# Gate sums by 128-column products, a bf16 zero state, and filler products moved to the head of the kernel

## The chip, the cores and the metric

The kernel runs on one core of one Trainium2 chip. The metric is the device time of one execution in microseconds (us); the time before is the median of three runs.

## What is computed

Two layers follow each other. The first is a gated recurrent attention (mLSTM) over 4 batches, 8 heads, 768 steps and head size 40; the second is a feed-forward layer over 3072 tokens, 320 to 2048 to 320, with a hard-swish.

```
m_new = maximum(f_gate + m, i_gate)
f_stab = exp(f_gate + m - m_new);  i_stab = exp(i_gate - m_new)
C = f_stab * C + i_stab * v k^T;   n = f_stab * n + i_stab * k
y = sigmoid(o_gate) * (C q) / max(|n q|, 1)
...
h = x @ w_in;  g = h * clip(h + 3, 0, 6) / 6;  out = g @ w_out
```

## The kernel before

**The attention** works in chunks of 128 steps, each cut in two halves of 64 (Q). In place of the step-by-step recurrence, running sums of the gates are made once per chunk range (`gates`), and a tile of decay factors of 128 x 256 per pair of heads (`gate`), exponentiated on ACT (L688). A `group` on PE makes the scores (part S, L720), the new state contributions (part K, L727) and the outputs (part B: the products with the carried state at L736, and with the weighted scores at L741). VectorE (DVE) and ScalarE (ACT) then finish: `front` (L755) multiplies scores and decay, `state` (L772 to L783) updates the state, `back` (L803, L805) sums the output, `fin` normalizes it, `turn` transposes it for the second layer. Work is cut in tasks: a task is a set of three (chunk, batch) pairs and half the heads. Tasks 0 and 1 have three groups each of kind S+K and of kind B, which use separate PSUM banks (xy, exy).

**The gate tiles of tasks 0 and 1** are not read back from memory as those of later tasks, but summed on PE (L662 to L667): an identity times a causal mask in bf16, and a selector matrix `sel` times the running sums in fp32. The two halves of the partitions are made by separate products, 64 columns each (`rows`), so that a half uses a quarter or less of the array. An fp32 product appears in the trace as two instructions.

**A state that doesn't exist yet** (first chunk of a batch) is read from a tile of fp32 zeros (`zero`, L730), with the same products as a real one. Eight B groups do that.

**The second layer** starts when the early pools are released (`open_moe`, event "mo"): `mm1` (L952) and `mm2` (L996 to L1000), with three fp32r products in place of one fp32. Its weights come packed and are decoded first on ACT and DVE (`weight_slice`, L866 to L911).

**The order of work** is fixed at build time: `Plan.run` steps through all jobs with costs of its own and due times, and each job writes its instructions as its step is reached. Each engine then runs its list in order, also SyncE (SP), which issues all DMAs. The plan's clock is not that of the chip. `T_WARM` (6.9) and `TF` (18.5) are times of the plan.

**Fillers.** The job `warm` has the last rank on PE: where the plan finds PE idle, from 18.5 on its clock until "mo", it writes one bf16 product of 128 x 512 zeros from the tile `ones` into a bank that nothing reads (L460). `ones` is cleared by GpSimd (POOL) as its first job (L455). POOL then makes `sel`, the mask and the identity with memsets and affine selects (L482 to L492), before its first step of the gates (L498).

Of the kernel before, what the change touches and what calls it, by code (L numbers as in the profile page):

```python
# [7 lines left out]
F32 = mybir.dt.float32  # L8
F32R = mybir.dt.float32r
BF16 = mybir.dt.bfloat16  # L10
# [4 lines left out]
ALU = mybir.AluOpType  # L15
# [4 lines left out]
L = 128  # L20
# [5 lines left out]
BH = B * H  # L26
BR = 2 * BH
E2 = D + 2
Q = 64
# [53 lines left out]
WN = 512  # L83
# [4 lines left out]
BL = 2.781  # L88
T_WARM = 6.9
TF = 18.5121  # L90
ENGINES = 'yddzwagdyxdadgddaapddddgyagadx'
BG = -2.7305
BA = -12.8028
# [78 lines left out]
class Plan:  # L172
# [4 lines left out]
    def __init__(self, slots):  # L177
        self.free = {e: 0.5 for e in "padgq"}
        self.free["a"] = 2.5
        self.dma = 0.5  # L180
        self.slots = {k: [(0.0, i) for i in range(n)] for k, n in slots.items()}
        self.done = {}
        self.jobs = []
        self.behind = {}
        self.held = {}
        self.opened = []
        self.nw = 0
        self.work = {}
        self.port = 0.0
        self.small = False  # L190
        self.shared = {}
        self.n = 0

    def add(self, due, gen, after=(), att=1, slack=None):
        self.n += 1
# [101 lines left out]
    def run(self):  # L297
        self.settle()
        while self.jobs:
            best = {}  # L300
            for j in self.jobs:
                e = j["req"][0]
                cost = j["req"][1]
                if e == "*":
                    fin = {o: self.ready(j, o, c) + c + {"a": BA, "d": BD, "g": BG}[o] for o, c in j["req"][1].items()}
                    e = min(fin, key=fin.get)
                    cost = j["req"][1][e]
                if e not in self.free:
                    continue
                start = self.ready(j, e, cost)  # L310
                if e == "p":
                    start = max(start, j["t"] + HOPP * (j["eng"] != e and j["att"]))
                if e == "q" and not j["first"]:
                    start = max(start, self.dma - BL)
                late = start > max(self.free[e], self.port if (e == "g" or isinstance(cost, Lock)) else 0.0) + j["slack"]
                k = (late, start if late else 0.0, j["due"] + (j["req"][2] if len(j["req"]) > 2 and e != "q" else 0.0), j["n"])
                if e not in best or k < best[e][0]:
                    best[e] = (k, start, j, e, cost)
            assert best, [(j["n"], j["due"], j["req"]) for j in self.jobs]
            _, start, j, e, cost = min(best.values(), key=lambda b: b[1])  # L320
            if e == "q":
                self.free[e] = start + (j["req"][2] if len(j["req"]) > 2 else 0.475)
                self.dma = max(self.dma, self.free[e] + DMA0) + cost
                j["t"] = self.dma + DMA
            else:
                end = start + cost
                if e == "p":
                    big = j["gen"].__name__ in ("mm1", "mm2")
                    if big and self.small:
                        cost = cost + 0.08  # L330
                    self.small = not big
                    end = self.stream(start, cost)
                elif e == "g" or isinstance(cost, Lock):
                    self.port = end
                self.free[e] = j["t"] = end
            j["eng"] = e
            self.resume(j, e)
            self.settle()
        assert not self.nw, list(self.behind)

# [36 lines left out]
def mlstm_moe_kernel(ctx: ExitStack, tc: tile.TileContext, ig, fg, qkd, natd, ond, w_in, w_out, ident_d, out):  # L377
    nc = tc.nc
# [16 lines left out]
    ones = cst.tile([128, max(WN, 128)], BF16, name="ones")  # L395
    half = cst.tile([128, 1], F32, name="half")
    mask = cst.tile([128, Q], F32, name="mask")
    zero = cst.tile([128, 2, E2], F32, name="zero")
# [5 lines left out]
    f_s = cst.tile([BR, GN * L], F32, name="f_s")  # L404
# [13 lines left out]
    plan = Plan(dict(wm=1, ez=0, xy=1, exy=1, z=1, es=1, eo=1, st=2, nat=2, gw=NGW, ht=2, on=1, x=2,  # L418
                     y=NY, raw=NRAW, lw=2, mm=2, acc0=1, acc1=1, acc2=1, g=2, gs=GS, ob=3, rd=3))
    put, event = plan.put, plan.event  # L420
    early, early_ctx = {}, {}
# [29 lines left out]
    def warm():  # L451
        got = yield "get", "wm"
        pw = early["ps"].tile([128, 512], F32, tag="wm", name="pw")
        yield "g", 0.1
        nc.gpsimd.memset(ones, 0.0)  # L455
        while "mo" not in plan.done:
            plan.now["t"] = max(plan.now["t"], TF)
            yield "p", mat(1, WN, four=False), 1.0e6
            if "mo" not in plan.done:
                nc.tensor.matmul(pw[:, :WN], ones[:, :128], ones[:, :WN], start=True, stop=True)  # L460

    sel = early["ea"].tile([BR, 12, Q], F32, name="sel")
    maskb = early["ea"].tile([128, Q], BF16, name="maskb")
    identb = early["ea"].tile([128, Q], BF16, name="identb")

    def load_ident():
        yield "q", kb(64, 300)
# [3 lines left out]
    def gates(c0, n):  # L471
# [5 lines left out]
        nc.sync.dma_start(f_s[:, :w], fg[:, cols])  # L477
        nc.sync.dma_start(i_s[:, :w], ig[:, cols])
        if c0 == 0:
            nc.vector.memset(one, 1.0)  # L480
            nc.vector.memset(one.rearrange("p (c t) -> p c t", t=Q)[:, :, 0:1], 0.0)
            nc.gpsimd.memset(sel, 1.0)  # L482
            for h in range(2):
                rs = slice(h * BH, h * BH + BH)
                nc.gpsimd.affine_select(sel[rs], sel[rs], pattern=[[-16, 2], [-1, 6], [0, Q]], compare_op=ALU.is_equal, fill=0.0, base=-8 * h, channel_multiplier=1)
            nc.gpsimd.memset(mask, 0.0)
            nc.gpsimd.memset(identb, 1.0)
            for h in range(2):
                rs = slice(h * Q, h * Q + Q)
                nc.gpsimd.affine_select(mask[rs], mask[rs], pattern=[[1, Q]], compare_op=ALU.is_ge, fill=NEG, base=0, channel_multiplier=-1)  # L490
                nc.gpsimd.affine_select(identb[rs], identb[rs], pattern=[[1, Q]], compare_op=ALU.is_equal, fill=0.0, base=0, channel_multiplier=-1)
            nc.gpsimd.tensor_copy(maskb, mask)  # L492
        f, i, m = f_s[:, :w], i_s[:, :w], m_s[:, 1 : w + 1]
        yield "d", ld(w)
# [1 line left out]
        b, t = (0 if c0 else 1), plan.now["t"]  # L496
        e = yield psub(26, w)
# [12 lines left out]
        t = plan.now["t"]  # L510
# [24 lines left out]
        e = yield pick(22, a=ca(32 * n), d=cd(32 * n))  # L535
        cast(e, gTs[:, :n], pc[:, 0])
        t = plan.now["t"]
# [33 lines left out]
    Cs = {}  # L571
# [73 lines left out]
    def gate(task, cp):  # L645
# [10 lines left out]
        if task < GBT:  # L656
            yield "wait", f"g_s{c}"
            gb = yield "get", "z", "eo", "ez"
            pb = bank(gb, [128, 2, 2, Q], f"gb{nm}")
            plan.now["t"] = max(plan.now["t"], T_WARM)  # L660
            yield "p", busy(1.0)
            rows = [(slice(h * Q, h * Q + Q), slice(h * BH, h * BH + BH)) for h in range(2)]  # L662
            for ho, _ in rows:
                nc.tensor.matmul(pb[ho], identb[ho], maskb[ho, None, None, :].broadcast_to([Q, 2, 2, Q]), start=True, stop=False)
            for j in range(2):
                for ho, hr in rows:
                    nc.tensor.matmul(pb[ho, j], sel[hr, 6 * quad + 2 * b + j], f_s[hr, c * L : c * L + L], start=False, stop=j == 1)  # L667
            src, slot = pb, gb
        else:
            if cp == 0:  # L670
                yield "wait", f"gsc{pair(u, U - 1)[0]}"
                t0 = plan.now["t"]
                for h in range(2):
                    plan.now["t"] = t0
                    yield "q", kb(197, 230), 0.6
                    nc.sync.dma_start(gt[h * Q : h * Q + Q].rearrange("p u j c t -> p (u j c t)"), gsc[quad, h, U * u : U * u + U].rearrange("n j t -> (n j t)")[None, :].partition_broadcast(Q))
                event(f"gl{nm}")
            else:
                yield "wait", f"gl{task}_0"
            e = yield pick(27, g=0.72, d=ld(256))  # L680
            E(e).tensor_tensor(gw, gw, mask[:, None, None, :].broadcast_to([128, 2, 2, Q]), ALU.add)
            src, slot = gw, None
# [16 lines left out]
    def group(g, parts):  # L699
# [9 lines left out]
        for kind, n in parts:  # L709
# [17 lines left out]
                            nc.tensor.matmul(xy[h * Q : h * Q + KM, c, 296 + j * E2 : 296 + j * E2 + E2], T["kn"][rs, o : o + KM], T["vn"][rs, cp, 2 * h + j], start=True, stop=True)  # L727
            else:
                st, gt, vh = T["st"][0], T["gw"][0], T["vh"]
                C0 = Cs.get((b, quad, ch - 1, 1), zero)  # L730
                C1 = Cs[(b, quad, ch, 0)]
                for j in range(2):
                    for h in range(2):
                        rs = slice(h * Q, h * Q + D)
                        for c in range(2):
                            nc.tensor.matmul(xy[c * Q : c * Q + Q, h, 212 + j * E2 : 212 + j * E2 + E2], st[rs, cp, j, 2 if c == h else 4], (C1 if c else C0)[rs, j], start=True, stop=True)  # L736
                for j in range(2):
                    for h in range(2):
# [429 lines left out]
```

## Time and profile before

| | us |
|---|---|
| median of three runs | 467.95 |
| the three runs | 467.95, 466.8, 472.23 |
| profiled execution, device time | 471.43 |
| its span (first to last instruction) | 469.7 |
| PE busy in the span | 456.3 (97%) |
| DVE, ACT, POOL busy | 304.9, 173.3, 179.2 |

The profiled execution took 1.7 us around its span. All times of the trace count from the span's start. PE's busy time is from modelled ends of pipelined products, so that a busy PE isn't one at its peak: the distance from one start to the next says more.

### The profile page before, as it was taken

The numbers are of one execution on the slowest core, as the hardware profiler recorded it, in microseconds if no ns is written. First come the engines' busy times: TensorE is split into PE (matmuls) and PEld (weight loads), VectorE is DVE, ScalarE is ACT, GpSimd is POOL, SyncE is SP. The second block draws the span as 40 slices with busy tenths as digits, with TensorE's granted clock in tenths as the row PEclk, the third lists the DMA queues.
The fourth block names the chain that finished last, engine by engine and source line by source line (L and its number), as shares of the span: only waits on it lengthen the run. The fifth ranks groups of instructions, "written<-read, shape, count | busy, mean of one in ns | idle before, by whom it ended". The sixth has DMA issues, their size and how long they took to land.

```text
span 469.7 us, 12926 instructions
## 1 busy us (share of the span) xinstructions
PE 456.3 (97%) x5407; PEld 419.7 (89%) x5407; DVE 304.9 (65%) x824; ACT 173.3 (37%) x352; POOL 179.2 (38%) x238
## 2 busy tenths in 40 slices
PE   4999899999999999999999999999999999999997
PEld 3756687878999999999999999999999999999996
DVE  2369999999998667864665736865844445623331
ACT  3547799945132322242222421242321411312221
POOL 4211502324645435442453534343543343242432
PEclk9999989999999999999999999999999999999999
DMA  6768874853614115421503313532403400001001
GB/s 226 276 207 223 295 233 160 295 176 99 188 31 155 55 37 180 150 78 43 172 16 128 101 43 128 169 116 66 164 0 94 143 4 2 1 0 43 0 1 42
DMA packets 25346, 53.36 MB, mean 114 GB/s; under 512 B 2184, under 2 KB 15304, under 8 KB 25288
## 3 DMA queue, kind: packets, MB, share of 16 engines
q1 hardware_dynamic: 25288, 52.54, 34.4%
q8 instruction: 42, 0.69, 0.6%
q14 instruction: 16, 0.13, 0.1%
HBM read 48.50 MB, written 4.03 MB: 112 GB/s over the span
## 4 chain that ended last, share of the span: by engine, by line
PE 82%; DVE 11%; ACT 4%; issue 1%; POOL 1%; POOLq 0%; ACTq 0%
PE h L952 34%; PE acc L998 11%; PE acc L999 11%; PE acc L1000 10%; PE xy L736 3%; PE xy L720 3%; PE xy L741 2%; PE xy L727 2%; PE xa L847 2%; PE pw L460 2%; PE gb L667 1%; DVE vr L893 1%; DVE yi L895 1%; DVE gw L690 1%; DVE wlo L911 1%
## 5 line engine op out<-in xcount | busy, mean ns | idle before, releaser
L979 POOL TENSOR_TENSOR gl<-g,gh 128x384 fp32r<-128x384 f32 x112 | 117.8, 1053 | 190.7 <-DVE gh L443 125.2
L969 ACT ACTIVATE g<-h,half 128x384 f32<-128x384 f32 x116 | 67.1, 580 | 185.4 <-PE h L952 180.6
L971 DVE SCALAR_TENSOR_TENSOR g<-g,h 128x384 f32<-128x384 f32 x116 | 63.9, 552 | 107.3 <-ACT g L969 107.2
L998 PE MATMUL acc<-vh,gh 128*128 128x320 f32 x336 | 104.7, 312 | 0.0
L999 PE MATMUL acc<-vl,gh 128*128 128x320 f32 x336 | 103.6, 308 | 0.0
L1000 PE MATMUL acc<-vh,gl 128*128 128x320 f32 x336 | 103.5, 308 | 0.0
L952 PE MATMUL h<-xh,whi 128*128 128x384 f32 x256 | 93.1, 364 | 2.3 <-DVE gv L971 2.3
L952 PE MATMUL h<-xh,wlo 128*128 128x384 f32 x256 | 86.7, 339 | 0.2 <-DVE wlo L911 0.2
L952 PE MATMUL h<-xl,whi 128*128 128x384 f32 x256 | 86.5, 338 | 0.0
L998 PEld LDWEIGHTS acc<-vh,gh 128*128 128x128 f32 x336 | 63.0, 188 | 0.2
L999 PEld LDWEIGHTS acc<-vl,gh 128*128 128x128 f32 x336 | 63.2, 188 | 0.0
L1000 PEld LDWEIGHTS acc<-vh,gl 128*128 128x128 f32 x336 | 63.0, 188 | 0.0
L952 PEld LDWEIGHTS h<-xh,whi 128*128 128x128 f32 x256 | 48.3, 189 | 5.3 <-DVE gv L971 2.5
L952 PEld LDWEIGHTS h<-xl,whi 128*128 128x128 f32 x256 | 48.4, 189 | 0.7
L952 PEld LDWEIGHTS h<-xh,wlo 128*128 128x128 f32 x256 | 48.3, 189 | 0.9 <-DVE wlo L911 0.9
L443 DVE CAST gh<-g 128x384 fp32r<-128x384 f32 x112 | 42.4, 382 | 5.1 <-DVE g L971 0.5
L952 PE MATMUL h<-xl,wtl 128*128 128x384 f32 x128 | 43.3, 338 | 0.0
L952 PE MATMUL h<-xh,wtl 128*128 128x384 f32 x128 | 43.2, 337 | 0.0
L642 POOL TENSOR_TENSOR nat<-nat,wT 128x168 f32<-128x168 f32 x48 | 25.4, 547 | 25.6 <-DMA nat<-in_nat_dram 14.8
L781 POOL TENSOR_TENSOR C<-C,dec 128x84 f32<-128x84 f32 x42 | 16.0, 381 | 38.0 <-ACT C L441 21.8
L692 ACT ACTIVATE gw<-gw 128x256 f32<-128x256 f32 x42 | 16.7, 415 | 31.2 <-DVE gw L690 31.0
L755 DVE TENSOR_TENSOR gw<-xy,gw 128x256 f32<-128x256 f32 x48 | 19.9, 415 | 9.4 <-PE xy L727 8.2
(112 smaller groups left out, 669.4 us busy)
## 6 DMA issues: line engine op xcount, KB each, us to landing
st<-in_qk_dram SPq DMA_DIRECT2D x15, 960.0 KB, 7.9
nat<-in_nat_dram SPq DMA_DIRECT2D x16, 504.0 KB, 4.4
gw<-gsc SPq DMA_DIRECT2D x28, 192.0 KB, 7.4
rawi<-in_w_in_dram SPq DMA_DIRECT2D x8, 640.0 KB, 5.2
rawo<-in_w_out_dram SPq DMA_DIRECT2D x8, 640.0 KB, 4.3
nat<-in_nat_dram SPq DMA_DIRECT2D x16, 252.0 KB, 4.5
on<-in_on_dram SPq DMA_DIRECT2D x8, 480.0 KB, 4.8
out_dram<-ob SPq DMA_DIRECT2D x24, 160.0 KB, 1.8
```

What stands on the lines that cost most here:

```text
L443: E(c).tensor_copy(dst, src)
L642: E(e).tensor_tensor(v, v, heads(wT[:, c], quad, b)[:, :, :, None].broadcast_to([128, 2, 2, E2]), ALU.mult)
L692: nc.scalar.activation(gw, gw, AF.Exp)
L755: nc.vector.tensor_tensor(gw, xy[:, :, 0:128].rearrange("p c (j t) -> p j c t", j=2), gw, ALU.mult)
L781: nc.gpsimd.tensor_tensor(Cn[:R], cur[:R], dc[:, :, None].broadcast_to([R, 2, E2]), ALU.mult)
L952: nc.tensor.matmul(hp, w, x, start=n == 0, stop=n == len(seq) - 1)
L969: nc.scalar.activation(g, hp, AF.Relu, bias=half, scale=1.0 / 6.0)
L971: nc.vector.scalar_tensor_tensor(g, g, 1.0, hp, ALU.min, ALU.mult)
L979: E(e).tensor_sub(gl, g, gh.bitcast(F32))
L998: nc.tensor.matmul(acc, gh[:, ts_], VH[f // 4][:, f % 4, :], start=f == 0, stop=False)
L999: nc.tensor.matmul(acc, gh[:, ts_], VL[p][:, f % 2, :], start=False, stop=False)
L1000: nc.tensor.matmul(acc, gl[:, ts_], VH[f // 4][:, f % 4, :], start=False, stop=f == NF - 1)
```

## The change

- `fill(n)` writes n filler products. Ten are written at the head of PE's list. In `Plan.run` one more is written behind each PE step of a job `gates`, `gate` or `group` as long as the plan's PE clock is under TE = 23.9. The job `warm` still takes its steps of the plan, but writes a product only where the plan's clock is past 23.9. So the order of all other instructions stays as it was.
- `ones` is cleared on DVE, not on POOL. Half of `sel` (now 128 columns per selector) and the identity (now 128 x 128) are preset by DVE memsets; POOL's two selects of `sel` have 64 partitions in place of 32; the two selects of the identity, 64 columns each, become one of 128.
- A gate tile is summed by three products with 128 columns in place of six with 64.
- Where no state exists, two bf16 products of zeros per group (84 columns each) take the place of the four fp32 products that read `zero`.

```diff
+TE = 23.9
...
+            if e == "p" and self.fill and j["gen"].__name__ in ("gates", "gate", "group") and self.free["p"] < TE:
+                self.fill(1)
...
-        nc.gpsimd.memset(ones, 0.0)
+        nc.vector.memset(ones, 0.0)
+        def fill(n):
+            for _ in range(n):
+                nc.tensor.matmul(pw[:, :WN], ones[:, :128], ones[:, :WN], start=True, stop=True)
+
+        plan.fill = fill
+        fill(10)
         while "mo" not in plan.done:
             plan.now["t"] = max(plan.now["t"], TF)
             yield "p", mat(1, WN, four=False), 1.0e6
-            if "mo" not in plan.done:
-                nc.tensor.matmul(...)
+            if "mo" not in plan.done and plan.now["t"] > TE:
+                fill(1)
...
+            nc.vector.memset(sel[:, :, Q:], 1.0)
+            nc.vector.memset(identb, 1.0)
...
-            nc.gpsimd.memset(sel, 1.0)
+            nc.gpsimd.memset(sel[:, :, :Q], 1.0)
...
-            nc.gpsimd.memset(identb, 1.0)
...
-                nc.gpsimd.affine_select(identb[rs], identb[rs], pattern=[[1, Q]], ...)
+            nc.gpsimd.affine_select(identb, identb, pattern=[[1, 128]], ...)
...
-            rows = [(slice(h * Q, h * Q + Q), slice(h * BH, h * BH + BH)) for h in range(2)]
-            for ho, _ in rows:
-                nc.tensor.matmul(pb[ho], identb[ho], maskb[ho, None, None, :]..., start=True, stop=False)
+            nc.tensor.matmul(pb, identb, maskb[:, None, None, :]..., start=True, stop=False)
             for j in range(2):
-                for ho, hr in rows:
-                    nc.tensor.matmul(pb[ho, j], sel[hr, 6 * quad + 2 * b + j], f_s[hr, ...], ...)
+                nc.tensor.matmul(pb[:, j], sel[:, 6 * quad + 2 * b + j], f_s[:, ...], ...)
...
-                C0 = Cs.get((b, quad, ch - 1, 1), zero)
+                C0 = Cs.get((b, quad, ch - 1, 1))
+                if C0 is None:
+                    for h in range(2):
+                        nc.tensor.matmul(xy[:Q, h, 212 : 212 + 2 * E2], ones[:, :Q], ones[:, : 2 * E2], start=True, stop=True)
...
-                        for c in range(2):
+                        for c in range(C0 is None, 2):
```

## Rows read from the trace of the kernel before

**Rows 1.** Busy time by stretch: start:end, length, engines, PEclk, DMA share, GB/s

```profile
6.54:22.50 15.96, 15.95 (x272) 12.18 (x273) 4.26 (x18) 7.65 (x32) 2.93 (x7) 1.00 0.80 291
21.71:34.45 12.74, 12.74 (x209) 6.93 (x202) 8.04 (x30) 6.43 (x11) 1.86 (x5) 1.00 0.63 207
34.45:113.00 78.55, 74.67 (x900) 58.17 (x899) 76.08 (x196) 61.76 (x122) 21.38 (x32) 0.98 0.70 223
200.00:250.00 50.00, 50.00 (x601) 48.70 (x600) 29.64 (x81) 14.28 (x28) 20.68 (x27) 1.00 0.23 70
```

**Rows 2.** The chain of waits, 0 to 46 us: start, length, engine and line

```profile
0.80 0.53 POOL ones L455
...
5.31 0.19 POOL identb L491
...
5.80 0.37 POOL i_s L498
...
6.56 0.29 PE pc L529
6.85 0.54 PE pc L533 x8
7.39 0.35 PE gb L664 x2
7.74 1.04 PE gb L667 x8
...
10.18 0.56 PE pc L552 x2
...
16.36 0.64 PE xy L720 x16
17.00 0.39 PE xy L727 x16
17.39 0.43 PE xy L736 x16
17.82 0.43 PE xy L741 x16
...
30.98 2.67 PE pw L460 x6
...
34.45 0.34 DVE ht L803
...
39.89 1.29 PE pw L460 x6
```

**Rows 3.** All instructions of line 460, the fillers: least, median and longest ns

```profile
L460 PE MATMUL pw<-ones x39: 379/379/634, 22.4 to 43.1; 128*128 128x512 bf16 x39
```

**Rows 4.** DVE in order of time, 0 to 30 us

```profile
1.07 0.27 DVE L480 MEMSET one<- 64x256 f32 x1
...
3.55 0.63 DVE L495 TENSOR_TENSOR_SCAN m_s<-f_s,i_s 64x128 f32<-64x128 f32 x1 [2.09 <-DMA i_s<-in_ig_dram]
...
26.98 0.33 DVE L803 TENSOR_TENSOR ht<-xy,eG 128x168 f32<-128x168 f32 x1 [1.11 <-PE xy L741]
```

**Rows 5.** PE in order of time, after 34 us: start, length, product, idle before

```profile
41.14 0.41 PE L552 MATMUL pc<-gTs,last 128*128 128x32 f32 x2
41.48 0.41 PE L556 MATMUL pc<-gTs,last 128*64 128x16 f32 x8
...
58.27 0.69 PE L952 MATMUL h<-xh,whi 128*128 128x384 f32 x1 [1.94 <-DVE gv L971]
...
299.79 0.44 PE L736 MATMUL xy<-C,st 40*64 40x42 f32 x16
...
300.28 0.44 PE L720 MATMUL xy<-st 40*64 40x64 f32 x16
...
300.86 0.44 PE L952 MATMUL h<-xh,whi 128*128 128x384 f32 x1
```

**Rows 6.** PE alone by stretch: busy, granted clock, DMA share, GB/s

```profile
59.00:60.00 1.00, 1.00 (x4) 0.50 0.51 198
```

More of the change, by code (lines that the diff above doesn't have):

```diff
@@ L192, in __init__ @@
         self.n = 0
+        self.fill = None
     def add(self, due, gen, after=(), att=1, slack=None):
@@ L458, in warm @@
             yield "p", mat(1, WN, four=False), 1.0e6
-            if "mo" not in plan.done:
-                nc.tensor.matmul(pw[:, :WN], ones[:, :128], ones[:, :WN], start=True, stop=True)
-    sel = early["ea"].tile([BR, 12, Q], F32, name="sel")
+            if "mo" not in plan.done and plan.now["t"] > TE:
+                fill(1)
+    sel = early["ea"].tile([BR, 12, 128], F32, name="sel")
     maskb = early["ea"].tile([128, Q], BF16, name="maskb")
-    identb = early["ea"].tile([128, Q], BF16, name="identb")
+    identb = early["ea"].tile([128, 128], BF16, name="identb")
     def load_ident():
@@ L479, in gates @@
         if c0 == 0:
+            nc.vector.memset(sel[:, :, Q:], 1.0)
+            nc.vector.memset(identb, 1.0)
             nc.vector.memset(one, 1.0)
             nc.vector.memset(one.rearrange("p (c t) -> p c t", t=Q)[:, :, 0:1], 0.0)
-            nc.gpsimd.memset(sel, 1.0)
+            nc.gpsimd.memset(sel[:, :, :Q], 1.0)
             for h in range(2):
-                rs = slice(h * BH, h * BH + BH)
-                nc.gpsimd.affine_select(sel[rs], sel[rs], pattern=[[-16, 2], [-1, 6], [0, Q]], compare_op=ALU.is_equal, fill=0.0, base=-8 * h, channel_multiplier=1)
+                cs_ = slice(h * Q, h * Q + Q)
+                nc.gpsimd.affine_select(sel[:, :, cs_], sel[:, :, cs_], pattern=[[-16, 2], [-1, 6], [0, Q]], compare_op=ALU.is_equal, fill=0.0, base=-8 * h, channel_multiplier=1)
             nc.gpsimd.memset(mask, 0.0)
-            nc.gpsimd.memset(identb, 1.0)
             for h in range(2):
@@ L490, in gates @@
                 nc.gpsimd.affine_select(mask[rs], mask[rs], pattern=[[1, Q]], compare_op=ALU.is_ge, fill=NEG, base=0, channel_multiplier=-1)
-                nc.gpsimd.affine_select(identb[rs], identb[rs], pattern=[[1, Q]], compare_op=ALU.is_equal, fill=0.0, base=0, channel_multiplier=-1)
+            nc.gpsimd.affine_select(identb, identb, pattern=[[1, 128]], compare_op=ALU.is_equal, fill=0.0, base=0, channel_multiplier=-1)
             nc.gpsimd.tensor_copy(maskb, mask)
@@ L661, in gate @@
             yield "p", busy(1.0)
-            rows = [(slice(h * Q, h * Q + Q), slice(h * BH, h * BH + BH)) for h in range(2)]
-            for ho, _ in rows:
-                nc.tensor.matmul(pb[ho], identb[ho], maskb[ho, None, None, :].broadcast_to([Q, 2, 2, Q]), start=True, stop=False)
+            nc.tensor.matmul(pb, identb, maskb[:, None, None, :].broadcast_to([128, 2, 2, Q]), start=True, stop=False)
             for j in range(2):
-                for ho, hr in rows:
-                    nc.tensor.matmul(pb[ho, j], sel[hr, 6 * quad + 2 * b + j], f_s[hr, c * L : c * L + L], start=False, stop=j == 1)
+                nc.tensor.matmul(pb[:, j], sel[:, 6 * quad + 2 * b + j], f_s[:, c * L : c * L + L], start=False, stop=j == 1)
             src, slot = pb, gb
```

## The prediction

> **What bounds the kernel now.** I read the busy times by stretch first, then the chain of waits, then single engines in order of time. The kernel has three parts. From 6.54 to 34.45 us PE's list sets the pace: in [rows 1] PE is busy for 15.95 of 15.96 us up to 22.50 while DVE has 4.26 and ACT 7.65, and the chain runs on PE from 6.56 to 34.45 almost without a break [rows 2]. From 34.45 to 113 DVE is busy 76.08 of 78.55 us. After that PE is full to the end (50.00 of 50.00 in the sample stretch) [rows 1]. An engine's list is fixed, so what comes earlier at 34.45 comes earlier everywhere behind, as long as DVE is then full and its inputs come earlier too.
>
> The point is how slow PE is in the first part. The PEclk column says 1.00 there [rows 1], but the spacing of equal products says otherwise: six fillers of 512 columns take 2.67 us at 30.98, 0.445 each, and 1.29 at 39.89, 0.215 each [rows 2]. That is 1.2 and 2.4 columns per ns, the two levels of 1.2 and 2.4 GHz. So PE runs at 1.2 GHz until about 34 us, and rises only behind that dense run of six full-array products. From 6.5 to 22.4 PE was busy too, with small tiles and no filler (the first is at 22.4, [rows 3]), and stayed low.
>
> **The start.** POOL stands on the chain from 0.80 until its step of the gates at 5.80 [rows 2]. It loses the clearing of `ones` (0.53) and the second select of the identity (0.19); the remaining one has twice the columns, which costs between 0 and another 0.19. So i_s is ready 0.5 to 0.7 earlier. The clearings of `ones`, half of `sel` and the identity go to DVE, which waits 2.09 us for a DMA before 3.55; by the memset of 64x256 in 0.27 [rows 4] the largest, three times as many columns, is about 0.8, and all three about 1.3. They are hidden; without that cover they would delay the scan by up to 1.3. The ten fillers start when `ones` is clear, about 1.5, and at 0.445 each end near 6.0, about where the earlier i_s now lets L529 start (6.56 less 0.6). I take 0.4 us off; bounds 0 and 0.7.
>
> **6.56 to 22.50 at the high clock.** Each piece of the chain [rows 2] against the same work later [rows 5]:
> - A gate tile takes 0.35 + 1.04 = 1.39. The change halves the number of instructions; two halves ran side by side, so the columns streamed stay the same. At the high clock: 0.20 for the mask (half of 0.35, rounded up), and four fp32 instructions at 0.17, from the pair of L552 with full-width weights (41.14 to 41.48). That is 0.88, within half of 1.39 (0.70) and no gain at all (1.39). Six gates: 3.1 off.
> - L529 with L533 0.83, L552 0.56 and the similar L556 (0.54 by L533): 1.93 in all, times 0.34/0.56, is 1.17: 0.8 off.
> - Four S+K groups, 1.03 each (0.64 + 0.39), take 0.58 (300.28 to 300.86): 1.8 off.
> - Two B groups, 0.86, take 0.49 (299.79 to 300.28): 0.7 off. The two bf16 zero products have no row in this form; they replace half of L736's work, but that half ran beside the other. Between 0.1 gained and 0.4 lost in both groups; I take 0.2 lost.
> - Thirteen fillers stand between these steps, at 0.215 each: 2.8 added. (Stepping through the plan of the kernel before, whose order stays, 18 steps of gates, gate and group end under 23.9, fourteen of them up to the fourth S+K group.)
>
> Sum: -3.1 - 0.8 - 1.8 - 0.7 + 0.2 + 2.8 = **-3.4 us**.
>
> **21.71 to 34.45.** DVE works 8.04 of 12.74 us here [rows 1] and idles 4.70, in five waits behind PE of which the one of 1.11 at 26.98 is typical [rows 4]. By the same stepping, 8 of the 39 fillers lie at or under 23.9: those in clusters of 2, 3, 1 and 2 in this stretch, 3.6 us at 0.445; five at 0.215 stand in their place. The six at 30.98 stay and take 1.29. PE then needs here three S+K and three B groups (3.2), eleven fillers (2.4) and a transpose or two: under 6.5, less than DVE's 8.04. So DVE sets the pace, and what stays of the idle time is the round trip from DVE through a group and back. Bounds: all 4.70 stays (0), or none (-4.7). At half the PE time I leave 0.4 to each of five waits: **-2.7 us**.
>
> Next late is DVE itself. DMAs are not: SP's weight loads wait for buffers that ACT frees in the same lists, and its gate load for chunk 1 waits for the last gate product, so both move along; DMA is at 0.63 in this stretch [rows 1].
>
> **Sum.** -0.4 - 3.4 - 2.7 = -6.5 us at 34.45. DVE carries it through to 113 (2.47 us of idle time in 78.55), PE from there. The profiled execution, 471.43 (span 469.7 and 1.7 around it), would become about 465.0. It lies 3.5 above the median of the three runs, 467.95; nothing in it says that the difference is the low clock, so I take the 6.5 off the median: **461.5 us**. The likeliest case's own range is 459 to 464.
>
> **Rivals.**
> 1. *The clock doesn't rise at the head, and the fillers stand in the way* (slower). It did not rise in 16 us of busy small tiles, nor behind the clusters of two and three fillers. It decides whether ten fillers, 4.4 us, are enough as six were; for it, the rise came behind the end of such a run, and the work that follows still has small tiles. Against it, ten are more than six. Price: thirteen fillers at 0.445 (+5.8), 0.4 off at the start, the gates as they were, and from the fourth group on eight fillers less and five more (-1.3): +4.1 at most; DVE's idle time may take back 2. About +3, 471.
> 2. *The clock rises, but the gain stops at the attention's head.* The DVE waits stay (0 in place of -2.7), or the clock falls again where fillers are dropped: after PE stood idle 1.94 us before 58.27 [rows 5] the granted clock was 0.50 [rows 6]. Then -3.8, less about one such dip: -2.5 to -3.8, about 465.
> The Trainium skill, "TensorE: Matmul & The Clock Gate", Part 1, says that the ramp's penalty is under 1% of a typical kernel's span and that one shouldn't fit to a count of cold products. By it the gain stays under 4.7 us (an estimate, 1% of the span), 463.3 or more. The trace disagrees on the extent: PE is low for about 28 us, 6% of the span.
> 3. *The gain is lost behind 34 us*, if a weight load becomes the bound where DMA already has a share of 0.70 [rows 1]; 466 to 469. For it: loads and decoding share three buffers. Against it: these loads wait for ACT, not ACT for them.
>
> **Chances.** Likeliest case 0.62, rival 1 0.14, rival 2 0.16, rival 3 0.08. What a measurement can tell from no change is about 1%, 4.7 us: under 463.3 or over 472.6. Faster: most of the likeliest case (0.51) and a little of rival 2 (0.04), 0.55. Slower: a third of rival 1 and something unforeseen, 0.08. Same: 0.37. The range from 458.8 to 469.5 takes in rivals 2 and 3, the upper part of the likeliest case's unknown bounds, and leaves out rival 1.
>
> **What would show it.** The fillers' spacing at the head: ten at 0.445, or the last ones at 0.215. The start of L529 near 6.1; gate to gate 1.1 including a filler (1.8 if the clock stayed low); the end of the fourth S+K group near 18.7; DVE's L803 of the fifth B group, now at 34.45, near 28; the first L952 near 37; DVE's idle time between 34 and 113 as before. I am wrong if that L803 is early and the end isn't, or if PE's spacing stays at 0.445.

## The result and the profile after

The changed kernel takes 467.42 us in the median (463.72 to 477.95), the kernel before 471.60 over as many executions (21, 466.8 to 474.99). The ratio is 0.9914, 95% interval 0.9889 to 0.9938: 0.86% faster, about 4.1 us. Forecast were 461.5 us and a gain of 6.5. The three executions that the forecast started from had a median of 467.95, 3.6 below that of the 21. The ratios, here and below, leave out a kernel's executions that took over 1.5% more than its fastest: of the changed kernel one of 470.80 and five of 476.7 to 478.0. But those five turn out to be rival 1 itself (below), and so belong to the change. Over all 21 executions the mean is 469.6, against 471.3 before: 1.7 us, which isn't clear of the noise (95% interval -0.5 to 4.0).

The first two profiles of the changed kernel fell on such an execution (477.19 and 477.03). A third, of 467.86 (span 466.1), shows the usual case; "the changed kernel" below means this profile unless the other is named. Its chain of waits, to be read against [rows 2]:

```profile
1.41 4.45 PE pw L462 x10
5.86 0.24 PE pc L539
6.10 0.11 PE pc L540
...
6.75 0.32 PE pw L462
7.07 0.11 PE gb L673
7.18 0.64 PE gb L675 x4
...
12.15 0.39 PE xy L728 x16
12.54 0.22 PE xy L735 x16
...
25.45 1.62 PE pw L462 x7
...
27.92 0.34 DVE ht L814
```

The ten fillers still run at 0.445 each. The filler behind the transposes takes 0.32 instead of the 0.54 that it takes in the other profile below, and a gate tile 0.11 + 0.64 = 0.75 in place of 1.39. DVE's step of the fifth B group, at 34.45 before, is at 27.92: 6.53 us earlier. All fillers, 59 against the 39 of [rows 3], whose first is at 22.4:

```profile
L462 PE MATMUL pw<-ones x59: 379/389/634, 1.4 to 36.5; 128*128 128x512 bf16 x59
```

PE in order of time, with the first product of the first layer, the stretch behind 47 us, and a product of the second unit (tile 1) that is at 112.90 before:

```profile
36.97 0.45 PE L963 MATMUL h<-xh,whi 128*128 128x384 f32 x1
...
51.74 0.69 PE L963 MATMUL h<-xh,whi 128*128 128x384 f32 x1 [1.94 <-DVE gv L982]
52.22 0.52 PE L963 MATMUL h<-xl,whi 128*128 128x384 f32 x1
52.54 0.52 PE L963 MATMUL h<-xh,wlo 128*128 128x384 f32 x1
...
54.60 0.69 PE L563 MATMUL pc<-gTs,last 128*128 128x64 f32 x2
...
57.62 0.99 PE L963 MATMUL h<-xh,whi 128*128 128x384 f32 x1
...
61.78 0.58 PE L963 MATMUL h<-xh,whi 128*128 128x384 f32 x1
...
109.32 0.45 PE L963 MATMUL h<-xh,whi 128*128 128x384 f32 x1
```

The first product is at 36.97; before it is at 43.50. At 109.32 the lead is 3.58. So 6.53 us are won up to 37 us and 2.95 of them are given back before 110. Busy times by stretch, to be read against [rows 1]: length, then PE, PEld, DVE, ACT, POOL, PEclk, DMA share and GB/s. The stretch from 19.30 to 27.92 holds the work of 21.71 to 34.45 before, and that from 27.92 to 109.32 the work of 34.45 to 112.90.

```profile
19.30:27.92 8.62, 7.67 (x188) 4.99 (x189) 7.45 (x30) 6.38 (x11) 2.16 (x5) 1.00 0.75 251
27.92:109.32 81.40, 77.85 (x881) 60.93 (x881) 76.25 (x196) 61.92 (x122) 21.94 (x32) 0.94 0.70 221
...
47.00:58.80 11.80, 9.86 (x55) 7.88 (x54) 10.42 (x23) 8.68 (x18) 4.52 (x5) 0.67 0.63 206
58.80:112.90 54.10, 53.10 (x730) 43.31 (x732) 50.83 (x134) 38.97 (x72) 15.46 (x23) 0.98 0.60 187
200.00:250.00 50.00, 50.00 (x598) 48.74 (x598) 29.03 (x80) 12.40 (x25) 20.20 (x25) 1.00 0.20 64
```

DVE, which worked 8.04 of 12.74 us in the first of these stretches before, now works 7.45 of 8.62: most of the idle time is gone. But behind it DVE idles 5.15 us, where it idled 2.47 before. From 47 to 58.8 alone DVE idles 1.38 us and PE 1.94, and the clock is low for much of it (0.67 in the mean). Behind an idle stretch of 1.94 us the products of 384 columns start 0.32 us apart, which is 1.2 columns per ns; at the high level they are 0.175 apart.

The same 27 products show what this costs. They run from 54.60 to 61.78 in the changed kernel and from 61.13 to 65.28 before; the first line is the changed kernel's, the second that of the kernel before:

```profile
54.60:61.78 7.18, 7.18 (x27) 5.86 (x27) 5.94 (x13) 5.19 (x10) 0.00 (x0) 0.54 0.82 238
```

```profile
61.13:65.28 4.15, 4.15 (x27) 3.48 (x27) 4.15 (x10) 4.05 (x8) 0.00 (x0) 0.99 0.77 219
```

PE is full in both and takes 3.03 us longer at a granted clock of 0.54 than at 0.99. So the 2.95 us are given back in this one place, to the low clock.

The other kind of execution (477.19), its chain of waits:

```profile
1.41 4.45 PE pw L462 x10
...
6.75 0.54 PE pw L462
7.29 0.21 PE gb L673
7.50 1.15 PE gb L675 x4
8.65 0.54 PE pw L462
...
21.23 0.35 PE xy L741 x2
...
39.80 0.34 DVE ht L814
```

Up to 6.75 nothing differs. Then each filler takes 0.54 and a gate 1.36: the clock did not rise. The step that is at 34.45 before comes at 39.80, 5.35 late, and the execution ends 5.8 us above the profiled one before.

### The profile page after: what moved, and what is told of

The parts are those of the page before. It is cut to its first block, busy times and chain, and to the rows that moved or that the text cites. A ratio compares the mean times of both kernels' runs of the same rounds, so it can differ in the third digit from the quotient of the medians.

```text
span 475.5 us, 12797 instructions
## 1 busy us (share of the span) xinstructions
PE 463.1 (97%) x5342; PEld 423.2 (89%) x5349; DVE 306.9 (65%) x827; ACT 173.2 (36%) x352; POOL 178.2 (37%) x235
## 4 chain that ended last, share of the span: by engine, by line
PE 83%; DVE 11%; ACT 5%; issue 1%; ACTq 0%
PE h L963 34%; PE acc L1009 11%; PE acc L1010 10%; PE acc L1011 10%; PE xy L747 3%; PE pw L462 3%; PE xy L728 3%; PE xy L752 2%; PE xy L735 2%; PE xa L858 2%; PE gb L675 1%; DVE vr L904 1%; ACT lwo L888 1%; DVE gw L698 1%; DVE yi L906 1%
```

## The experiments

All ratios are against the kernel before, run beside the variant on the same chip. "Lead" is how much earlier than before a product of the first layer starts, from the profile of the variant.

**Is it the clock, and are ten fillers enough?**

*e1, the changed kernel again* (no edit).

> The changed kernel itself, for a profile of an execution of the usual length. Theory A (the time hangs on whether TensorE's clock rises during the ten head fillers): the spacing of fillers falls from 0.445 to 0.215 us before about 7 us, the fourth S+K group ends near 19 us, and the time is about 467; an execution in which the spacing stays at 0.445 until 37 us takes about 477. Rival B (the clock doesn't matter, the gain is POOL's earlier start): 467 also with a spacing of 0.445.

466.55 us, ratio 0.9892 (0.9855 to 0.9930). Of nine executions seven lie between 464.3 and 467.3, two at 477.0 and 478.1; none between.

*e2, fourteen at the head.*

```diff
-        fill(10)
+        fill(14)
```

> Fourteen head fillers in place of ten, all else as changed. Theory A: four more at 0.445 make a run of 6.2 us, so that the clock rises at the head in nearly all executions; none near 477, median 465 to 467 (the four cost at most 4 x 0.445 = 1.8 us where the clock is late, 0.9 us or less where it has risen). Rival B: 1 to 2 us longer than with ten, and the spread up to 477 stays.

466.70 us (462.70 to 469.67), ratio 0.9906 (0.9872 to 0.9940). None of twelve executions is near 477. The fourteen take 4.76 us, hardly more than the ten in 4.45, because the last ones run at the high clock. Lead at the first product 6.39. Theory A holds, and the median lies within its 465 to 467. Against the kernel before, the mean over all executions falls by 4.0 us, with ten (e1) by 2.0.

*e7, four at the head.*

```diff
-        fill(10)
+        fill(4)
```

> The changed kernel with four head fillers in place of ten, those behind the steps kept. Theory A: the clock stays at the low level in all executions until about 37 us, and the fillers behind the steps stand in the way: 475 to 478. Rival F (the fillers behind each step lift the clock by themselves, a little later): 466 to 470.

477.51 us (476.73 to 479.95), ratio 1.0167 (1.0112 to 1.0222): 1.7% slower, in every execution. This is rival 1 made permanent. Fillers behind the steps don't lift the clock; they cost time while it is low.

Counted over all, by their time: 8 of 32 executions of the changed kernel (ten fillers) stayed low (476 or more), all 4 with four fillers, and none of the 68 of the six kernels with fourteen at the head and fillers behind the steps (highest 472.75).

**Which part of the change does it?**

*e4, the change without its fillers* (gates by 128 columns, bf16 zero state, memsets moved).

```diff
...
-        plan.fill = fill
-        fill(10)
...
-            if "mo" not in plan.done and plan.now["t"] > TE:
-                fill(1)
+            if "mo" not in plan.done:
+                nc.tensor.matmul(pw[:, :WN], ones[:, :128], ones[:, :WN], start=True, stop=True)
```

> The change without its fillers (gate tiles by 128-column products, bf16 zero state, memsets and selects moved; fillers as before, none at the head). Theory A: the clock stays low until about 34 us as before; only POOL's 0.5 us and nothing of the gates: 470.5 to 472, against 471.6 for the kernel before. Rival B: 467.

471.73 us, ratio 1.0025 (0.9991 to 1.0059): no gain. PE in order of time in its profile:

```profile
5.80 0.31 PE L534 MATMUL pc<-ident,i_s 32*128 32x32 f32 x1 [0.22 <-DVE i_s L523]
...
6.58 0.39 PE L667 MATMUL gb<-maskb,identb 128*128 128x256 bf16 x1
6.90 1.22 PE L669 MATMUL gb<-f_s,sel 64*128 64x128 f32 x4
8.05 0.40 PE L667 MATMUL gb<-maskb,identb 128*128 128x256 bf16 x1
```

A gate of whole products takes 1.47 us at the low clock; the halves took 1.39 [rows 2]. POOL's part shows (the transposes of i_s start at 5.80, at 6.56 before), and is worth nothing at the end.

*e3, the fillers alone* (ten; gates, zero state, memsets of the masks as before).

```diff
-            nc.tensor.matmul(pb, identb, maskb[:, None, None, :]..., start=True, stop=False)
...
+            rows = [(slice(h * Q, h * Q + Q), slice(h * BH, h * BH + BH)) for h in range(2)]
+            for ho, _ in rows:
+                nc.tensor.matmul(pb[ho], identb[ho], maskb[ho, None, None, :]..., start=True, stop=False)
...
-                C0 = Cs.get((b, quad, ch - 1, 1))
+                C0 = Cs.get((b, quad, ch - 1, 1), zero)
...
```

> The fillers of the change alone (ten at the head, one behind each early step, none of the plan's before 23.9, the filler tile cleared on DVE); gate tiles by 64-column products, the fp32 zero state and POOL's memsets and selects as before. Theory A: the clock rises at the head as in the changed kernel; what the products do after it must show whether it stays up with gates of 64 columns. If it stays up, 467 to 468 (0.3 us more for POOL); if gates of 64 columns let it fall, 470 to 475. Rival B: 471 to 475, since POOL's part is missing.

464.48 us, ratio 0.9861 (0.9818 to 0.9905). Of six executions four lie between 463.3 and 465.3, two at 470.5. The whole gain is there without the rest of the change. Gates of 64 columns don't let the clock fall as long as a filler stands behind each:

```profile
6.80 0.30 PE L674 MATMUL gb<-maskb,identb 64*64 64x256 bf16 x2
7.03 0.65 PE L677 MATMUL gb<-f_s,sel 32*64 32x128 f32 x8
7.62 0.39 PE L462 MATMUL pw<-ones 128*128 128x512 bf16 x1
7.93 0.30 PE L674 MATMUL gb<-maskb,identb 64*64 64x256 bf16 x2
```

Gate to gate 1.13 us here, 1.07 in the changed kernel. This profile was one of 470.47, in which the clock fell again at 25 us, after a stretch in which PE had little to do: PE from 20 to 24 us is busy 2.09 of 4.00, and the granted clock from 28 to 32 is 0.52.

*e5, the fillers alone with fourteen* (`fill(14)` in e3).

> The fillers alone, with fourteen at the head. Theory A (clock at the head): as fillers alone with ten, 463 to 466, and no execution that stays at 0.445 spacing. Theory C (what is missing of the forecast gain is lost to low clock behind the head): executions spread over 463 to 470 with the mean granted clock, about 1 us per 0.0035 of it. Rival D (128-column gates and bf16 zero state help once the clock is up): 1 us or more above the changed kernel with fourteen, 466.7.

465.18 us, ratio 0.9883 (0.9848 to 0.9918). Its lead at the first product is the longest, 7.00. Rival D expected 467.7 or more, and e5 came 1.5 us below e2 instead. Its interval overlaps that of e2, so whether the gate and zero parts cost or gain stays open. Theory C holds over the executions: the four with a mean granted clock of 1.000 took 463.55 to 465.0, that with 0.982 took 471.15.

*e10, the zero state in fp32 again, fourteen at the head.*

```diff
-        fill(10)
+        fill(14)
...
-                C0 = Cs.get((b, quad, ch - 1, 1))
-                if C0 is None:
-                    for h in range(2):
-                        nc.tensor.matmul(xy[:Q, h, 212 : 212 + 2 * E2], ones[:, :Q], ones[:, : 2 * E2], start=True, stop=True)
+                C0 = Cs.get((b, quad, ch - 1, 1), zero)
...
-                        for c in range(C0 is None, 2):
+                        for c in range(2):
```

> The changed kernel with fourteen head fillers, and the zero state in fp32 as before. If the bf16 zero products cost 0.2 to 0.3 us in each early B group (0.26 in the chain at 15.00 us), the first layer product comes 0.3 to 0.6 us earlier than with them, and the time is 466.0 to 466.5, against 466.7; if they cost nothing, no difference at that product.

466.59 us, ratio 0.9909 (0.9873 to 0.9944), the same as e2; the first product came 0.5 us later than in e2, not earlier. The bf16 zero products buy and cost nothing that these runs can tell.

*e11 and e12, no fillers behind the steps* (fourteen at the head, the plan's fillers as before; e11 with gates of 64 columns and the fp32 zero state, e12 with both changed).

```diff
-        plan.fill = fill
-        fill(10)
+        fill(14)
...
-            if "mo" not in plan.done and plan.now["t"] > TE:
+            if "mo" not in plan.done:
```

> Gate products and zero state as before; fourteen fillers at the head, none behind the steps, the plan's fillers as before. Theory A with the clock held by the fillers behind: the clock rises at about 5 us, falls again within the gates of 64 columns, and stays low until the plan's fillers: 468 to 471. If the clock stays up without them: 462 to 464, since 13 x 0.32 us leave PE's path.

> The change with fourteen fillers at the head and none behind the steps, the plan's fillers as before. If products of 128 columns hold the clock up where those of 64 do not, the clock stays up through the gates here and the time is 463 to 466; if both fall, 468 to 472 as with gates of 64 columns.

466.02 us, ratio 0.9896 (0.9834 to 0.9957), and 464.74, 0.9859 (0.9790 to 0.9928), each from four executions; one of e12's took 474.59. PE alone by stretch in e12's profile (busy, granted clock, DMA share, GB/s):

```profile
5.00:10.00 5.00, 5.00 (x42) 1.00 0.92 304
10.00:11.00 1.00, 0.96 (x20) 0.95 1.04 387
12.00:18.00 6.00, 6.00 (x91) 0.50 1.04 416
18.00:24.00 6.00, 5.99 (x146) 0.74 0.49 168
```

The clock falls at 10.9 us while PE is full with gates and groups, also with gates of 128 columns; in e11 it falls at 11.3. So wide gates don't hold it, and the expectation that they would is refuted, though e12's time looked well.

*f3, e12 again, with more executions.*

> The change with fourteen fillers at the head and none behind the steps, again. Theory A: 464 to 466 in most executions, ratio to the kernel before 0.984 to 0.989; executions in which the clock falls early and stays low until the plan's fillers 470 to 475. Whether it beats the changed kernel (0.9914 and 0.9892) is open: I expect 2 us at most.

470.68 us (465.63 to 475.61), ratio 0.9993 (0.9958 to 1.0028). With twelve executions nothing is left of e12's gain. The time goes with the granted clock: the three executions at 0.982 or more took 465.6 to 467.0, the seven at 0.970 to 0.974 took 469.4 to 471.5, the two below took 474.8 and 475.6. The filler behind each step is what keeps the clock: with it, e2, e5, e9 and e10 have 1.00 in every stretch up to 33 us. It does not do so in every profile (e3 above; in e6 the clock falls near 26 us). And these two kernels keep the plan's eight early fillers as well, which cost time by themselves (e9 below), so that their time is not the price of the clock alone.

**Where does the lead go behind 47 us?**

*f1 and f2, the changed kernel, one execution each.*

> The changed kernel, a look. If the clock rises at the head: ten fillers in 3.5 to 4.5 us, the first layer product near 37 us (lead of 6 to 6.5 against 43.50), and at 113 us a lead of 4 to 5, less where the clock fell for 6.8 us near 52, near 6 where it fell for 3.4 or not at all. If it doesn't: the first product near 48.8 as in the first profile.

> The same kernel and expectation as f1; a second look, since about one execution in four has stayed at the low clock.

467.86 and 478.59 us. f1 is the profile shown with the result; f2 stayed low.

*e6 and e8, 38 small products where PE idles near 50 us* (e6: on e2; e8: on e5).

```diff
+        def mid(k):
+            for _ in range(k if c0 == 2 else 0):
+                nc.tensor.matmul(pc[:, 3:5], ones[:, :128], ones[:, :128], start=True, stop=True)
+
+        mid(20)
         event(f"gates{c0 + n}")
...
         yield "p", busy(0.75)
+        mid(18)
```

> The changed kernel with fourteen head fillers, and 38 more products of 128 columns of zeros in the third range of gates (20 behind its transposes, 18 ahead of its last products, into columns that the last products overwrite), where PE idles 1.2 and 1.1 us near 50 and 53 us. Theory C: the granted clock no longer falls near 52, the first-layer products behind keep the lead of 6.4 us that they have at 47 us, and the time is 464 to 465, against 466.7 without. Rival E (the lead is lost to DVE and ACT, which wait for each other there; the low clock only shows it): the clock stays up and the time is 466 to 467 all the same.

> The fillers alone with fourteen at the head and the 38 products in the third range of gates. Theory C: 462 to 464, the shortest of all. Rival E: as without the 38.

467.51 us, ratio 0.9944 (0.9906 to 0.9982), and 466.38, 0.9900 (0.9858 to 0.9942). In both profiles the clock did stay up there, and the time didn't follow: theory C is refuted in its times. In e8 PE and the waits between 40 and 62 us show where time went:

```profile
50.39 1.29 PE L546 MATMUL pc<-ones 128*128 128x128 bf16 x20
51.98 0.45 PE L968 MATMUL h<-xh,whi 128*128 128x384 f32 x1 [0.30 <-DVE gv L987]
...
54.84 1.17 PE L546 MATMUL pc<-ones 128*128 128x128 bf16 x18 [1.20 <-ACT eG L560]
```

```profile
DVE m_s L505 <- DMA i_s<-in_ig_dram: 1.4, 1, 1.4
PEld L546 <- issue: 1.4, 2, 1.3
PE pc L546 <- ACT eG L560: 1.2, 1, 1.2
```

The second batch waits 1.20 us for the same ACT step as the products behind it, and so adds its 1.0 us to the path. And here the gates' third range came late from memory: DVE waited 1.4 us for it, and PE 0.85 behind it. In e5 the same wait is 1.9 us, and 1.35 on PE. So these two variants, which have the longest leads, don't tell the low clock and rival E apart.

*e9, the plan's early fillers kept* (on e5).

```diff
-            if "mo" not in plan.done and plan.now["t"] > TE:
+            if "mo" not in plan.done:
```

> The fillers alone, fourteen at the head, one behind each early step, and the plan's eight fillers before 23.9 kept as well. Theory C (low clock behind the head takes back a part): the dip near 25 us that some executions show, where PE is thin from 19 to 25 us, doesn't come; executions lie within 462 to 467, median 464. Rival G (these fillers stand in front of the groups): the first layer product is 0.5 us or more later than without, median 465.5 or more.

467.03 us, ratio 0.9939 (0.9904 to 0.9974). Rival G is right: the first product comes 1.9 us later than in e5 (lead 5.09 against 7.00).

**The leads side by side.** Start of tile 4 and tile 8 of the first unit (before: 53.40 and 72.26, 18.86 apart), from the profiles, with the time for which the granted clock was 0.50 between 47 and 65 us:

| profile | lead at the first product | low for | tile 4 to tile 8 | lead at 456 us |
|---|---|---|---|---|
| before | 0 | 3.4 | 18.86 | 0 |
| e9 | 5.09 | 0 | 17.95 | 4.27 |
| e10 | 5.86 | 0 | 18.78 | 5.34 |
| e12 | 6.20 | 3.4 | 19.20 | 6.88 |
| f3 | 4.60 | 3.4 | 18.32 | 5.20 |
| e2 | 6.39 | 6.8 | 20.57 | 4.52 |
| e3 | 2.53 | 6.8 | 20.17 | 0.99 |
| e11 | 2.90 | 6.8 | 20.30 | 1.92 |
| e5 | 7.00 | 6.8 | 21.87 | 3.89 |
| f1 (changed) | 6.53 | 10.2 | 22.09 | 3.60 |
| e6, mid fill | 3.72 | 0 | 19.96 | 2.81 |
| e8, mid fill | 6.81 | 0 | 20.32 | 4.62 |

The table is read within the unfilled variants: low for 0 or 3.4 us, the stretch takes 18 to 19 us, as before, and the lead stays; low for 6.8, 20.2 to 21.9, where the upper end, e5, holds the late load told of above; low for 10.2, 22.1. e4, without a lead, was low for 10.2 there as well, and lost 3.1. The 24 executions of the changed kernel that did not stay low at the head say the same by their mean granted clock: five at 1.000 took 463.7 to 464.8, eight near 0.993 took 466.3 to 467.5, six at 0.989 (f1 is one) 467.2 to 468.7, two at 0.985 469.5 and 470.8. The rows of the changed kernel and, behind them, of e10, PE alone by stretch:

```profile
52.00:56.00 4.00, 4.00 (x19) 0.50 0.41 115
56.00:60.00 4.00, 4.00 (x10) 0.50 0.90 246
```

```profile
52.00:56.00 4.00, 2.45 (x19) 1.00 0.38 149
56.00:60.00 4.00, 4.00 (x19) 1.00 0.95 236
```

From 56 to 60 us e10 gets through 19 products where the changed kernel gets through 10.

## Why the prediction was right and wrong

**What bounds the kernel before** was read rightly. e4 and e7 show it from both sides: the changed gates and zero state without a clock that rises at the head gain nothing (e4) or lose 1.7% (e7), and the fillers alone gain all (e3, e5).

**The start.** L540 joins the chain at 6.10, L529 was at 6.56: 0.46 off, 0.4 forecast. DVE's memsets were hidden.

**6.56 to 22.50.** 3.4 forecast; the filler behind the fourth S+K group starts at 19.84 where the fillers before started at 22.50 in the chain, so that with the start 2.7 are won, not 3.8. The gate was over-priced (0.75, not 0.88), the S+K group about right (0.61, not 0.58), the B group with its zero products under-priced (0.79, not 0.59). The filler was under-priced most: 0.32 in the chain, with what lies between two kinds of products, not 0.215. Thirteen of them make 1.4 us more than forecast; the six gates give 0.5 of it back, and the groups take 0.4.

**21.71 to 34.45.** 2.7 forecast, and 4.1 came: DVE goes from its first step of the stretch to L814 in 8.62 us (19.30 to 27.92) where it took 12.74. I left 2.0 us of waits; 1.2 stayed. The two misses cancel, which is luck, and the sum of -6.5 at this point is what f1 shows (-6.53). e2, e5, e8 and e10 give -6.39, -7.00, -6.81 and -5.86 at the first product, 9 us later, so f1's own figure is not one odd execution.

**"DVE carries it through to 113 ... PE from there"** is the step that failed. DVE was full there before, and I took its 2.47 us of idle time for a constant. It is not, it became 5.15: near 50 us PE waits for DVE (1.94 us of PE idle before 58.27 in [rows 5], and the same 1.94 in the changed kernel), the clock falls there, and how long it stays low differs from execution to execution, 0 to 10.2 us in these profiles, 3.4 in that of the kernel before. While it is low, PE sets the pace again (7.18 of 7.18 us busy from 54.60 to 61.78, while DVE idles 1.24). Of the 6.53 us, 2.95 went there in f1. In e10, where the clock stayed up, 0.5 went; in e12, low for 3.4 as the kernel before, nothing. The prediction had named this sign of being wrong: L803 early and the end not. It had also read the dip of the kernel before ([rows 6]) and put one in rival 2, at up to 1.3 us, but not that the dip can last three times as long as in the kernel before. What decides its length is not settled. Fillers there kept the clock up and the time did not fall (e6, e8), so that rival E (DVE and ACT wait for each other anyway) may have a part in it too; that is not shown.

**The baseline.** I took 6.5 off a median of three executions, 467.95. The profiled execution, 471.43, was the better sample: 21 executions have 471.60, and the later medians are 470.1 to 472.0. From 471.60 the forecast would have been 465.1. So of the 5.9 us between 461.5 and 467.42, 3.6 are the baseline and 2.3 the lead that was lost. The prediction saw nothing to say that the 3.5 us between the two is the low clock; the record does point that way. Of the 89 further executions of the kernel before, the 15 with a mean granted clock of 1.000 have a median of 467.87, the 21 with 0.996, as the profile has, 471.57. One thing stays open here: against those 467.87 the changed kernel's five at 1.000 (median 464.32) gain 3.6 us and not 6.5. The column can't show the level ahead of the first change of the clock, so such executions of the kernel before may have risen earlier at the head; no trace of one was kept.

**Rival 1** was right in kind, had a fair chance (0.14 against 8 of 32), and was under-priced: +3 forecast, about +6 measured (e7 1.0167, some 7.8 us), since a filler costs 0.54 and not 0.445 between other products, and because DVE took nothing back. **Rival 3** (a late load) is seen in two variants, though it is a load of the gates and not of weights: DVE waits 1.9 us for it in e5 and 1.4 in e8. **Rival 2** is nearest to what the usual execution does, in its second form, the clock that falls again; DVE's waits of the head, its first form, did not stay. The Trainium skill, "TensorE: Matmul & The Clock Gate", Part 1, warned that the ramp's penalty is under 1% of a typical kernel's span and that one shouldn't fit to a count of cold products. By the time it came out so, 0.86%; by mechanism not: the low stretch at the head was worth 6.5 us (1.4% of 471) at its end, and the loss came from another low stretch. That a count is a poor guide is borne out: ten fillers lifted the clock in 24 of 32 executions, with the same products at the same times up to 6.75 us.

## What to carry to other kernels

Read the clock level from the spacing of equal products: the PEclk column said 1.00 up to 34 us, while PE ran at half speed ([rows 1], [rows 2]). A gain made at the head by a higher clock must be followed through every later stretch in which PE idles, and a kernel's own dips belong in the baseline; one profile shows one outcome of several. Filler products pay when there are enough of them at the head to work each time (fourteen rose in all 68 executions, ten in 24 of 32, and the fourteen cost nothing that shows), and when something keeps the clock up behind them; where they miss, each is a cost, and the executions that miss belong in the account.

## What the runs showed of the hardware that I had not expected

- In the changed kernel, between gates and groups, a filler of 512 columns takes 0.54 us of the chain at the low clock and 0.32 at the high one; back to back 0.445 and 0.215 ([rows 2]).
- PE full with small tiles is no protection: in e12 it was busy 5.00 of 5.00 us from 5 to 10 with the clock at 1.00, and 6.00 of 6.00 from 12 to 18 with the clock at 0.50.
- A gate tile by four whole products (64x128) is slower than by eight half ones at the low clock, 1.47 against 1.39 us, and a little faster at the high one (1.07 against 1.13 with its filler).
